# Second layer's output product as Strassen's seven products over 256-token blocks, its weights staged as float32 in DRAM

## The chip, the cores and the metric

One core of a Trainium2 chip runs the kernel. The metric is the device time of one execution in microseconds; the time before is 1062.11 us, the median of three runs. TensorE (PE) multiplies matrices and writes to PSUM; VectorE (DVE), ScalarE (ACT) and GpSimd (POOL) work on elements; SyncE (SP) issues the transfers.

## The reference

Three stages follow each other: a delta-rule attention over 768 steps, and two dense layers over its 3072 tokens.

```python
for t in range(S):                       # S = 768, 4 batches, 8 heads, 48 wide
    y[:, :, t] = einsum('bhd,bhde->bhe', q[:, :, t], state)
    v_old = einsum('bhde,bhd->bhe', state, kt)
    state = state + bt * einsum('bhd,bhe->bhde', kt, vt - v_old)
x = y as [3072, 384]
h = x @ w1_in;  x = (max(h, 0) + log1p(exp(-|h|))) @ w1_out   # 384 -> 2048 -> 384
h = x @ w2_in;  out = (h * cos(h)) @ w2_out                   # 384 -> 2048 -> 384
```

## The kernel before

**Numbers.** Each float32 operand of a product is split into two float16 parts, hi and lo (lo is what hi leaves), and a product is the sum of three matmuls, hi by hi, hi by lo and lo by hi (PAIRS). The weights arrive as 64-bit words; `conv` (L437) loads a 768 KB piece (128 hidden features of both weight matrices), turns it to float32 with three integer operations on DVE and a scaling on ACT or DVE, and makes hi and lo. `weights(0)` and `weights(1)` (L421) do that for the 16 pieces of each layer; `weights(1)` can begin only once the tiles of the attention's preparation are given up (`open_wp2`, L954, key `wp2`).

**Stages.** The attention works in 24 chunks of 32 steps (`step`, L696), prepared four at a time (`norms`, `prep`, `solve`). After two chunks, 256 tokens are ready for the first layer: `moe_block(0, j)`, 12 blocks of 8 units, a unit being two hidden pieces of 128 features. The second layer, `moe_block(1, j)`, runs 6 blocks of 512 tokens by 16 units of one hidden piece. A unit is an input product (`moe_in`, L784), the elementwise work that makes g and its hi and lo, and an output product (`moe_out`, L845) that accumulates in PSUM over the block's units. `moe_end` (L868) empties the accumulators: for the first layer into DRAM (`x2d`), for the second to the output.

**The second layer's unit.** The input product is 9 matmuls (3 pieces of 384 features by 3 pairs) of 128 by 512 into one of five PSUM banks (`hring`). DVE adds and subtracts a magic number (L835, L401), ACT takes the absolute value and the sine (L406, L408), DVE multiplies (L401), ACT or DVE copies hi (`copy`, L385), POOL or DVE subtracts for lo (`tt`, L397). The output product is 9 matmuls of 512 columns (3 pieces of 128 output features by 3 pairs) into three banks (`acc2`).

**Order.** Every operation is handed to `put` with the engines that may run it and an estimated cost, and with the keys that it writes and reads. `Plan` puts all of them into one fixed order per engine before the run, by a list scheduling forwards and backwards over those costs; in its model DVE operations marked `port` and POOL operations exclude each other. At run time each engine follows its order and waits by semaphores. All transfers are issued by SP, in order. The attention has a small priority boost, and the layers fill TensorE between its steps.

## Time and profile before

| | us |
|---|---|
| median of three runs | 1062.11 (1055.21 to 1067.48) |
| the profiled execution, device time | 1063.94 |
| its span in the trace | 1062.1 |
| TensorE busy in the span | 946.3 |
| DVE, ACT, POOL busy | 656.2, 681.4, 404.0 |

The profile shows one execution. Busy times of TensorE's matmuls include the length of its pipeline, so the pace is read from the starts of following instructions, not from their durations. Times in a timeline count from the start of the span. An instruction's line can be that of a helper (L397 is every tensor-tensor operation, L401 every scalar-tensor-tensor, L385 every copy).

### The profile page before, as it was taken

The page shows a single profiled execution, that of the slowest core. Times are in us where ns is not written, and L with a number is a line of the kernel's source. Part 1 is how long each engine was busy: PE and PEld are TensorE (multiplying, and loading weights), DVE is VectorE, ACT ScalarE, POOL GpSimd, SP SyncE. Part 2 cuts the span into 40 slices and gives each one's busy share as a digit, 9 for nine tenths or more (in the row PEclk, how much of TensorE's full clock was granted, in tenths as well). Part 3 has the DMA queues.
Part 4 walks back from the last instruction along what each step waited for, and adds up shares of the span by engine and source line. Part 5 has one row for each costly group of instructions (what it writes and reads, how often), then busy time and mean ns, then how long its engine had stood idle before and what let it go on. Part 6 is the DMA issues. An engine that isn't in the chain of part 4 may idle for free.

```text
span 1062.1 us, 27812 instructions
## 1 busy us (share of the span) xinstructions
PE 946.3 (89%) x11552; PEld 687.3 (65%) x11552; DVE 656.2 (62%) x1146; ACT 681.4 (64%) x1281; POOL 404.0 (38%) x365
## 2 busy tenths in 40 slices
PE   1246769898889899999999999999999999999998
PEld 1146648797778789889988998844444444444443
DVE  7876877566836683674485675497555555555554
ACT  5455748686757676777666877976555545555554
POOL 7363526433423352252223433555223323223332
PEclk9556978999989999999999999999999999999999
DMA  8888794758754876567477972111101000010000
GB/s 246 217 219 173 162 246 113 178 129 181 174 127 69 178 170 121 84 156 168 68 148 178 215 169 83 60 45 60 60 1 60 1 30 30 1 60 1 30 1 31
DMA packets 307742, 117.94 MB, mean 111 GB/s; under 512 B 272160, under 2 KB 287648, under 8 KB 307616
## 3 DMA queue, kind: packets, MB, share of 16 engines
q1 hardware_dynamic: 307616, 116.17, 46.2%
q8 instruction: 91, 1.49, 0.6%
q14 instruction: 35, 0.29, 0.1%
HBM read 71.03 MB, written 35.65 MB: 100 GB/s over the span
## 4 chain that ended last, share of the span: by engine, by line
PE 63%; DVE 9%; DMA 8%; SPq 7%; ACT 6%; issue 4%; POOL 2%; DVEq 0%; POOLq 0%; ACTq 0%
PE psH L798 18%; PE accA L860 12%; PE accB L860 9%; PE psC L798 7%; SPq L376 7%; PE psA L860 6%; PE psC L679 5%; PE psY L798 3%; PE psY L679 2%; DMA kt<-k_dram 2%; DMA bdA<-kq 1%; DMA kpd<-kp 1%; PE psA L589 1%; DVE tmpd L397 1%; DVE tlan L397 1%
## 5 line engine op out<-in xcount | busy, mean ns | idle before, releaser
L397 POOL TENSOR_TENSOR g<-g,g 128x512 f16<-128x512 f32 x192 | 227.4, 1185 | 499.1 <-ACT g L385 489.1
L798 PE MATMUL psH<-xt,w 128*128 128x256 f16 x1728 | 238.2, 278 | 7.6 <-DVE g L397 5.9
L385 ACT ACTIVATE g<-g 128x512 f16<-128x512 f32 x192 | 120.5, 629 | 104.4 <-DVE g L401 65.4
L798 PEld LDWEIGHTS <-w 128*128 128x128 f16 x1728 | 159.5, 99 | 28.3 <-issue 8.1
L860 PEld LDWEIGHTS <-w 128*128 128x128 f16 x1728 | 162.8, 98 | 21.2 <-issue 1.6
L860 PE MATMUL accA<-g,w 128*128 128x256 f16 x1152 | 159.0, 275 | 1.1 <-POOL g L397 1.0
L860 PEld LDWEIGHTS <-v 128*128 128x128 f16 x864 | 84.5, 98 | 102.1 <-issue 0.3
L798 PEld LDWEIGHTS <-v 128*128 128x128 f16 x864 | 84.5, 98 | 101.4 <-issue 0.8
L406 ACT ACTIVATE e<-e 128x512 f32<-128x512 f32 x96 | 60.3, 629 | 84.0 <-DVE e L401 84.0
L397 DVE TENSOR_TENSOR g<-psH,e 128x512 f32<-128x512 f32 x96 | 66.1, 688 | 67.1 <-ACT e L408 59.6
L860 PE MATMUL accB<-g,w 128*128 128x256 f16 x576 | 95.0, 275 | 0.0
L798 PE MATMUL psH<-xu,v 128*128 128x512 f16 x351 | 83.3, 379 | 0.6 <-DVE g L401 0.6
L798 PE MATMUL psC<-xu,v 128*128 128x512 f16 x342 | 81.5, 379 | 0.0
L679 PE MATMUL psC<-b,bdT 128*128 128x48 f16 x1152 | 44.1, 186 | 38.3 <-ACT bdT L385 18.9
L860 PE MATMUL accA<-g,v 128*128 128x512 f16 x288 | 78.0, 379 | 0.0
L860 PE MATMUL accB<-g,v 128*128 128x512 f16 x288 | 77.8, 379 | 0.0
L860 PE MATMUL psA<-g,v 128*128 128x512 f16 x288 | 77.6, 379 | 0.0
L679 PEld LDWEIGHTS <-bdKQ 128*128 128x128 f16 x1840 | 64.9, 99 | 15.1 <-issue 12.8
L815 ACT ACTIVATE e<-psH 128x512 f32<-128x512 f32 x96 | 56.8, 591 | 24.5 <-PE psH L798 23.6
L408 ACT ACTIVATE e<-e,hpi 128x512 f32<-128x512 f32 x96 | 69.1, 721 | 2.9
L679 PEld LDWEIGHTS <-bdT 128*128 128x128 f16 x1152 | 41.6, 99 | 42.2 <-issue 38.0
L679 PEld LDWEIGHTS <-bdA 128*128 128x128 f16 x1680 | 55.1, 99 | 9.1 <-issue 7.2
(128 smaller groups left out, 1550.0 us busy)
## 6 DMA issues: line engine op xcount, KB each, us to landing
bdKQ<-kqd SPq DMA_DIRECT2D x184, 64.0 KB, 2.9
kpd<-kp SPq DMA_DIRECT2D x24, 448.0 KB, 3.9
kqd<-kq SPq DMA_DIRECT2D x20, 512.0 KB, 4.5
raw<-w_dram SPq DMA_DIRECT2D x12, 768.0 KB, 6.0
bdA<-kpd SPq DMA_DIRECT2D x96, 96.0 KB, 3.7
w<-w_dram SPq DMA_DIRECT2D x10, 768.0 KB, 6.3
v<-w_dram SPq DMA_DIRECT2D x10, 768.0 KB, 4.8
qt<-q_dram SPq DMA_DIRECT2D x24, 256.0 KB, 3.7
```

The source lines that it names most:

```text
L376: put([("SP", issue)], w, r, lambda e: nc.sync.dma_start(out=dst, in_=src), dma=eng_us, **kw)
L385: nc.scalar.activation(out=out, in_=in_, func=AF.Copy, scale=scale)
L397: put(var, w, r, lambda e: eng[e].tensor_tensor(out=out, in0=a, in1=b, op=op), port=True, **kw)
L406: nc.scalar.activation(out=out, in_=in_, func=func, scale=scale)
L408: nc.scalar.activation(out=out, in_=in_, func=func, scale=scale, bias=bias)
L589: nc.tensor.matmul(ps[:, h], lhsT=w, rhs=x, start=(i == 0), stop=(i == len(ops) - 1))
L679: nc.tensor.matmul(ps[:, h, 0:D], lhsT=lhs(h), rhs=mov[:, h], start=(first and i == 0 and h == 0), stop=(last and i == len(passes) - 1 and ...
L798: nc.tensor.matmul(hp[:, i] if ph == 0 else hp, lhsT=w[:, l, kc * P:(kc + 1) * P], rhs=xv[:, m * KC + kc], start=(kc == 0 and idx == 0), s ...
L815: nc.scalar.activation(out=ev, in_=hv, func=AF.Abs, scale=sc)
L860: nc.tensor.matmul(acc[c], lhsT=w[:, l, c * P:(c + 1) * P], rhs=rhs, start=(f == 0 and idx == 0 and (ph == 1 or c != 1)), stop=(f == NF - ...
```

## The change

The second layer now works in 12 blocks of 256 tokens by 8 units of two hidden pieces, like the first. Its input product takes 18 matmuls of 256 columns. Its output product is Strassen's scheme over halves of the tokens, of the two hidden pieces, and of the 384 outputs: seven products of 128 tokens by 128 features by 192 outputs instead of eight. Here the combinations of g (`z`, 128 by 128) are the stationary operand and the combinations of the weights (192 columns) the moving one; each product is three matmuls, 21 a unit. They accumulate in seven halves of four banks (`acc2`); four banks are left for the input products. `moe_in` makes five sums or differences of quarters of g (`gx`) and hi and lo of all seven operands; `moe_end` combines the seven accumulators with copies and six multiply-adds into one tile and one 384 KB transfer.

The weights of the second layer: `early2`, put behind `weights` in the first layer, runs the 64-bit to float32 conversion and stores the result in DRAM (`w2d`). `weights2`, put in front of the last block of the first layer, loads it back in pairs of pieces and makes hi and lo of the input weights, the combinations of the output weights and their hi and lo. Several new tiles lie where earlier stages have theirs: the key `late` stands for the end of the attention's use, `late2` for the end of the first layer's use of its g tiles. The output's layout in DRAM becomes token by feature.

```diff
-NB2 = NS // 4
-NT = 2 * P, 4 * P
+NB = NS // 2
+NT = 2 * P
+DH = DM // 2
...
     hring = ([(ps_h[i], [("psH", i)]) for i in range(2)],
-             [(flat[i][0], [flat[i][1]]) for i in (1, 2, 4, 5, 6)])
-    acc2 = [flat[3], flat[7], flat[0]]
+             [(x.rearrange("p (a t) -> p a t", a=2), [k]) for x, k in (flat[i] for i in (1, 2, 4, 5))])
+    acc2 = [flat[i] for i in (0, 6, 3, 7)]
+    spare = bdA2.rearrange("p n b t -> p (n b t)")
+    raw2 = [spare[:, 4 * DM * 2 * i:4 * DM * 2 * (i + 1)].bitcast(I64).rearrange("p (o n) -> p o n", o=2) for i in range(2)]
+    gx = [spare[:, 6144 + 1280 * i:6144 + 1280 * (i + 1)].bitcast(F32).rearrange("p (k t) -> p k t", k=5) for i in range(2)]
+    gx16 = [x[:, 0:14 * P].rearrange("p (m k t) -> p m k t", m=2, k=7) for x in (
+        g16t.rearrange("p n a i t -> p (n a i t)"), bdT.rearrange("p h b t -> p (h b t)"),
+        bdG.rearrange("p h b t -> p (h b t)"))]
...
+    w2d = dr.tile([NFP, P, 2, 2, DM], I32, name="w2d")
...
+    def early2():
+        for f in range(NF):
+            cv, ck = cvb[f % NCV], [("cv", f % NCV)]
+            conv(w2, f, lambda: raws[0], [("raw", 0)], [], lambda cv=cv: cv, ck)
+            dma(w2d[f // 2, :, f % 2], cv, [("w2d", f // 2, f % 2)], ck, 1.09)
...
+    def weights2():
+        WP = [("wp2",)]
+        for p in range(NFP):
+            late = [("late",)] if p > 4 else []
+            at = PLACE[p]
...
+            put([("SP", 0.475)], ck, [("w2d", p, 0), ("w2d", p, 1)] + (WP if at == "x" else [("late",)] if at in "st" else []),
+                lambda e, p=p, pair=pair: nc.sync.dma_start(out=pair(), in_=w2d[p]), dma=2.18)
+            split(lambda p=p: win[0][:, 2 * p:2 * p + 2, 0], lambda p=p: win[0][:, 2 * p:2 * p + 2, 1],
+                  lambda pair=pair: pair().bitcast(F32)[:, :, 0], [("wi", 2 * p), ("wi", 2 * p + 1)], ck + WP + late, 2 * DM)
+            CV = ck + WP + late
...
+            for k, k2, a, b, op in ((0, 2, (A_, A_, 0), (A_, A_, 1), ALU.add), (2, 3, (A_, 0, 0), (A_, 1, 1), ALU.add),
+                                    (3, 4, (A_, 0, 1), (A_, 1, 1), ALU.subtract),
+                                    (4, 5, (A_, 0, 0), (A_, 1, 0), ALU.subtract)):
+                n = (k2 - k) * DH
...
+            for j, (k, n, x, r) in enumerate((
+                    (0, 3, lambda: wtmp[0][:, 0:3], [("wt", 0), ("wt", 2)]), (3, 1, lambda y=y: y((A_, 1, 1)), CV),
+                    (4, 1, lambda y=y: y((A_, 0, 0)), CV), (5, 2, lambda: wtmp[0][:, 3:5], [("wt", 3), ("wt", 4)]))):
...
+                put([("ACT", act(m)), ("DVE", dve(m, True))], key if j == 0 else key[1:], r + WP + late + ([] if j == 0 else key[:1]),
+                    lambda e, hl=hl: hl(e, 0), port=True)
+                put([("POOL", pool(m)), ("DVE", dve(m))], key[1:], r + WP + key[:1], lambda e, hl=hl: hl(e, 1), port=True)
...
+    PROD = ((0, 1), (2, 3), (4, 5), (6,))
...
+            q = gv.rearrange("p f (t n) -> p f t n", t=2)
+            x_, z = gx[s], gx16[s3]
+            L = [("late",), ("late2",)]
+            tt(x_[:, 0:2], q[:, :, 0], q[:, :, 1], ALU.subtract, [("gx", s, 0)], gk + L, 2 * P)
+            tt(x_[:, 3:5], q[:, 0], q[:, 1], ALU.add, [("gx", s, 3)], gk + L, 2 * P)
+            tt(x_[:, 2], q[:, 0, 0], q[:, 1, 1], ALU.add, [("gx", s, 2)], gk + L, P, only=("DVE",))
+            a = gv[:, 0, 0:P]
+            own = AP(a.tensor, a.offset, [a.ap[0], [3 * P, 2], a.ap[1]])
+            XK = [("gx", s, i) for i in (0, 2, 3)]
+            ZK = [("z", s3, i) for i in range(4)]
+            copy(z[:, 0, 5:7], own, 1.0, ZK[:1], gk + L, 2 * P)
+            tt(z[:, 1, 5:7], own, z[:, 0, 5:7], ALU.subtract, ZK[1:2], gk + ZK[:1], 2 * P)
+            copy(z[:, 0, 0:5], x_, 1.0, ZK[2:3], XK + L, 5 * P)
+            tt(z[:, 1, 0:5], x_, z[:, 0, 0:5], ALU.subtract, ZK[3:4], XK + ZK[2:3], 5 * P)
...
+            z = gx16[s3]
+            for (bank, key), ks in reversed(list(zip(acc2, PROD))):
+                def fn(e, bank=bank, ks=ks):
+                    for k in ks:
                         for idx, (l, m) in enumerate(PAIRS):
-                            rhs = g16[:, m, i] if ph == 0 else g16[:, m].rearrange("p a t -> p (a t)")
                             nc.tensor.matmul(
-                                acc[c], lhsT=w[:, l, c * P:(c + 1) * P], rhs=rhs,
-                                start=(f == 0 and idx == 0 and (ph == 1 or c != 1)),
-                                stop=(f == NF - 1 and idx == 2 and (ph == 1 or c != 0)))
-                us = 3 * len(cs) * mm(NT[ph])
+                                bank[:, DH * (k % 2):DH * (k % 2 + 1)], lhsT=z[:, m, k], rhs=wo(u)[:, l, k],
+                                start=(u == 0 and idx == 0 and k == ks[0]),
+                                stop=(u == NFP - 1 and idx == 2 and k == ks[-1]))
+                us = 3 * len(ks) * mm(DH)
                 moe_left[0] -= us
-                put([("PE", us)], [key], [("g16", s3, 0), ("g16", s3, 1), ("w", ph, f, 1)], fn, base=moe_left[0])
+                put([("PE", us)], [key], [("z", s3, i) for i in range(4)] + [("wx", u, i) for i in range(4)], fn,
+                    base=moe_left[0])
...
+            sc = 2.0 * math.pi / (G2_SC * W_SC)
+            o = wbuf[j % 2].bitcast(F32).rearrange("p o n -> p (o n)")[:, 0:2 * DM].rearrange("p (t c) -> p t c", t=2)
+            M = [acc2[k // 2][0][:, DH * (k % 2):DH * (k % 2 + 1)] for k in range(7)]
+            mk = [[acc2[k // 2][1]] for k in range(7)]
+            ok = [[("o", j % 2, i)] for i in range(4)]
+            old = [("w", 2 * (j % 2) + i, a) for i in range(2) for a in range(2)] if j < 2 else []
+            diag = AP(o.tensor, o.offset, [o.ap[0], [DM + DH, 2], [1, DH]])
+            def both(x):
+                return x.unsqueeze(1).to_broadcast([P, 2, DH])
+            copy(diag, both(M[2]), sc, ok[0] + ok[3] + old, mk[2], DM, ps=True)
+            copy(o[:, 0, DH:], M[3], sc, ok[1], mk[3] + ok[0], DH, ps=True)
+            copy(o[:, 1, 0:DH], M[4], sc, ok[2], mk[4] + ok[0], DH, ps=True)
+            for k, sg, dst, qs in ((3, -1, o[:, 0, 0:DH], (0,)), (1, 1, o[:, 0, 0:DH], (0,)), (4, -1, o[:, 1, DH:], (3,)),
+                                   (0, -1, o[:, 1, DH:], (3,)), (5, 1, o[:, :, DH:], (1, 3)), (6, -1, o[:, :, 0:DH], (0, 2))):
+                m = M[k] if len(qs) == 1 else both(M[k])
+                stt(dst, m, sg * sc, dst, ALU.mult, ALU.add, [x for i in qs for x in ok[i]], mk[k], DH * len(qs))
+            dma(out[j], o, [("out", j)], [x for i in ok for x in i], 1.09, issue=0.65)
...
+    weights()
+    early2()
...
+            if n == NS - 1:
+                put([("-", 0.0)], [("late",)] + [x for k in ("bdK", "bdQ", "bdA", "bd2", "bdT", "bdG") for x in bk(k)], (),
+                    lambda e: None)
+                weights2()
...
+    put([("-", 0.0)], [("late2",)] + [("g16", i, k) for i in range(NG16) for k in range(2)], (), lambda e: None)
```

## Rows read from the trace of the kernel before

The groups stand in the order in which the prediction comes to them. Times are microseconds from the span's start; L is a line of the kernel.

**Rows 1.** Busy times on the page: engine, us (share of the span), instructions

```profile
PE 946.3 (89%) x11552; PEld 687.3 (65%) x11552; DVE 656.2 (62%) x1146; ACT 681.4 (64%) x1281; POOL 404.0 (38%) x365
```

**Rows 2.** Windows of 50 us: busy us (instructions) by engine, PEclk, DMA share, GB/s

```profile
350.00:400.00 50.00, 46.01 (x785) 41.24 (x783) 37.16 (x84) 37.35 (x84) 23.42 (x26) 0.97 0.76 177
750.00:800.00 50.00, 50.00 (x233) 22.65 (x232) 26.60 (x40) 26.36 (x41) 13.90 (x12) 1.00 0.04 16
```

**Rows 3.** Timeline of TensorE, 640 to 700 us: start, length, engine, line, operation, count

```profile
641.67 0.57 PE L679 MATMUL psY<-u,bdA 128*128 128x48 f16 x16
642.08 0.49 PE L798 MATMUL psH<-xt,w 128*128 128x256 f16 x3
...
662.84 2.13 PE L798 MATMUL psH<-xt,w 128*128 128x256 f16 x18
664.80 0.82 PE L860 MATMUL accA<-g,w 128*128 128x256 f16 x6
...
697.54 0.81 PE L860 MATMUL accA<-g,v 128*128 128x512 f16 x3
```

**Rows 4.** Timeline of all engines, 1035 us to the end

```profile
1057.08 1.46 PE L860 MATMUL psA<-g,v 128*128 128x512 f16 x6
...
1058.57 0.60 ACT L385 ACTIVATE w<-psA 128x512 f32<-128x512 f32 x1 [0.70 <-PE psA L860]
```

**Rows 5.** Timeline of all engines, 753 to 775 us

```profile
759.23 2.11 PE L798 MATMUL psH<-xu,v 128*128 128x512 f16 x9
...
761.21 0.63 ACT L385 ACTIVATE g<-g 128x512 f16<-128x512 f32 x1 [0.89 <-DVE g L401]
...
761.91 1.16 POOL L397 TENSOR_TENSOR g<-g,g 128x512 f16<-128x512 f32 x1 [2.80 <-ACT g L385]
762.10 0.69 DVE L401 SCALAR_TENSOR_TENSOR e<-e,psH 128x512 f32<-128x512 f32 x1
...
763.11 2.11 PE L798 MATMUL psC<-xu,v 128*128 128x512 f16 x9
763.48 0.72 ACT L408 ACTIVATE e<-e,hpi 128x512 f32<-128x512 f32 x1
```

**Rows 6.** Groups by form, whole span: busy us, mean ns | idle before, releaser

```profile
L860 PEld LDWEIGHTS <-v 128*128 128x128 f16 x864 | 84.5, 98 | 102.1 <-issue 0.3
...
L467 POOL TENSOR_TENSOR v<-cv,v 128x768 f16<-128x768 f32 x16 | 28.3, 1768 | 9.2 <-ACT v L462 9.2
...
L401 DVE SCALAR_TENSOR_TENSOR u<-psC,u 128x384 f16<-128x384 f32 x48 | 26.5, 553 | 38.1 <-ACT u L385 38.0
...
L397 POOL TENSOR_TENSOR kp<-pm,kp 128x256 f16<-128x256 f32 x24 | 18.9, 789 | 29.2 <-ACT kp L385 27.0 <-PE psC L679 2.2
```

**Rows 7.** Timeline of DVE, then POOL, 700 to 740 us

```profile
705.58 1.53 DVE L454 SCALAR_TENSOR_TENSOR cv<-v,cv 128x768 int32<-128x768 int32 x1
...
715.25 0.67 DVE L835 TENSOR_SCALAR e<-psY 128x512 f32<-128x512 f32 x1
715.85 0.94 DVE L454 SCALAR_TENSOR_TENSOR cv<-raw,cv 128x768 int32<-128x768 int32 x1
...
705.14 1.16 POOL L397 TENSOR_TENSOR g<-g,g 128x512 f16<-128x512 f32 x1 [2.26 <-ACT g L385]
```

**Rows 8.** Window of 20 us: busy us (instructions) by engine, PEclk, DMA

```profile
700.00:720.00 20.00, 19.98 (x94) 8.97 (x93) 17.68 (x26) 14.78 (x22) 11.79 (x9) 1.00 0.11 38
```

**Rows 9.** DMA issues on the page: count, KB each, median us to landing

```profile
raw<-w_dram SPq DMA_DIRECT2D x12, 768.0 KB, 6.0
...
out_dram<-w SPq DMA_DIRECT2D x18, 256.0 KB, 2.0
```

**Rows 10.** Instructions on the second layer's weights: ns min/median/max, first and last start

```profile
L439 SPq DMA_DIRECT2D v<-w_dram x10: 328/388/524, 571.4 to 681.2; - x10
```

**Rows 11.** Chain of work that ended last, 300 to 400 us, by line

```profile
by line: SPq L376 21.0%; PE psH L798 15.5%; PE accA L860 9.8%; PE psC L679 8.5%; DMA kpd<-kp 5.3%; PE accB L860 4.9%; DMA kt<-k_dram 3.7%; PE psY L679 3.4%; DMA bdA<-kq 3.3%; issue 3.3%; DMA bdT<-tgd 2.6%; PE psA L589 2.6%; DVE g L397 2.0%;
```

More of the change, by code (lines that the diff above doesn't have):

```diff
@@ L311, in delta_moe_moe_kernel @@
     NG16 = 3
-    g16b = [moe.tile([P, 2, 2, 2 * P], F16, name=f"g16{i}") for i in range(NG16)]
+    g16t = moe.tile([P, NG16, 2, 2, 2 * P], F16, name="g16")
+    g16b = [g16t[:, i] for i in range(NG16)]
     xsb = moe.tile([P, KC, 2 * P], F32, name="xs")
@@ L464, in hi, with flo @@
                 nc.vector.tensor_copy(out=o_, in_=cf)
-        def lo(e):
-            eng[e].tensor_tensor(out=wview(ph, f)[:, :, 1], in0=cf, in1=wview(ph, f)[:, :, 0], op=ALU.subtract)
-        put([("ACT", act(n)), ("DVE", dve(n, True))], wk, ck, hi, port=True)
-        put([("POOL", pool(n)), ("DVE", dve(n))], wk, ck, lo, port=True)
+        def flo(e):
+            (h_, l_), cf = (x() if callable(x) else x for x in (hi, lo)), src()
+            eng[e].tensor_tensor(out=l_, in0=cf, in1=h_, op=ALU.subtract)
@@ new lines, in split, with conv, half, scale @@
+        put([("ACT", act(n)), ("DVE", dve(n, True))], wk, ck, fhi, port=True)
+        put([("POOL", pool(n)), ("DVE", dve(n))], wk, ck, flo, port=True)
+    def conv(w, f, t, key, r, cv, ck):
+        put([("SP", 0.475)], key, r, lambda e: nc.sync.dma_start(out=t(), in_=w[f]), dma=2.18)
+        n = 2 * DM
+        def half(b):
+            return t().bitcast(I32).rearrange("p o (n two) -> p o n two", two=2)[:, :, :, b]
+        put([("DVE", dve(n, True))], ck, key, lambda e: nc.vector.tensor_scalar(
+            cv(), half(1), 0x07FFFFFF, 3, op0=ALU.bitwise_and, op1=ALU.logical_shift_left), port=True)
+        put([("DVE", dve(n))], ck, key, lambda e: nc.vector.scalar_tensor_tensor(
+            cv(), in0=half(1), scalar=-0x40000000, in1=cv(), op0=ALU.bitwise_and, op1=ALU.bitwise_or), port=True)
+        put([("DVE", dve(n))], ck, key, lambda e: nc.vector.scalar_tensor_tensor(
+            cv(), in0=half(0), scalar=29, in1=cv(), op0=ALU.logical_shift_right, op1=ALU.bitwise_or), port=True)
+        def scale(e):
+            x = cv().bitcast(F32)
+            if e == "ACT":
+                nc.scalar.activation(out=x, in_=x, func=AF.Copy, scale=W_SC)
+            else:
+                nc.vector.tensor_scalar_mul(x, x, W_SC)
+        put([("ACT", act(n)), ("DVE", dve(n, True))], ck, [], scale, port=True)
@@ L832, in moe_in @@
             tt(gv, hv, ev, ALU.add, gk, hk + ek, n, only=("DVE",))
+            copy(g16[:, 0], gv, 1.0, [("g16", s3, 0)], gk, n)
+            tt(g16[:, 1], gv, g16[:, 0], ALU.subtract, [("g16", s3, 1)], gk + [("g16", s3, 0)], n)
         else:
@@ L895, in moe_block @@
             x, xk = (lambda: xt2[j % 2]), [("xt2", j % 2)]
-            put([("SP", 0.475)], xk, [("x2d", 2 * j), ("x2d", 2 * j + 1), ("wp2",)],
-                lambda e: nc.sync.dma_start(out=xt2[j % 2], in_=x2d[j]), dma=2.18)
-        NU = (NFP, NF)[ph]
-        for u in range(NU):
+            put([("SP", 0.475)], xk, [("x2d", j), ("wp2",)],
+                lambda e: nc.sync.dma_start(out=xt2[j % 2], in_=x2d[j]), dma=1.09)
+        for u in range(NFP):
             moe_in(ph, j, u, xk, x)
@@ L902, in moe_block @@
                 moe_out(ph, j, u - 2)
-        for u in range(NU - 2, NU):
+        for u in range(NFP - 2, NFP):
             moe_out(ph, j, u)
```

160 lines of the change are left out of this document (87 added, 73 removed).

## The prediction

> **What bounds the kernel now.** I read the page's busy times first, then the windows, then the timeline of one stretch. On the page TensorE is busy 946 of 1062 us and no other engine over 64% [rows 1]. The windows say where that is a limit. At 350 to 400 us TensorE is idle 4 us of 50, because the attention steps wait for each other; at 750 to 800 us it is not idle at all, at granted clock 1.00, the 2.4 GHz level [rows 2]. The second layer is of that second kind: its first output product starts at 697.54 [rows 3], its last six matmuls at 1057.08 [rows 4]. In the timeline the reader should see a strict rhythm: 18 matmuls of 512 columns (9 of the input product and 9 of the output product, between them) from 759.23 to 763.11, one unit of 512 tokens and 128 hidden features in 3.88 us, with ACT, POOL and DVE following inside it [rows 5]. What is taken from TensorE in this stage comes off the end of the kernel, if the others keep up.
>
> **TensorE.** A new unit is 256 tokens by 256 hidden features, the same work, so 96 units stay 96. Its input product is 18 matmuls of 256 columns, a form that the first layer has: 18 from 662.84 to 664.80, 108.9 ns each [rows 3], 1.96 us. Its output product is 7 products by 3 hi/lo pairs, 21 matmuls of 192 columns with a new 128-column weight load each; the trace has no such form. From above it is bounded by the 108.9 ns of 256 columns, from below by the 48-column form, 16 in 0.41 us, 25.6 ns each, each with its own weight load too [rows 3]. 512 columns take 3.88/18 = 215.6 ns, so a column costs (215.6 - 108.9)/256 = 0.417 ns and 192 columns 82.2 ns. That value I take, since the 48-column row shows that loads of this size don't set the pace down to 26 ns. The unit: 1.96 + 21 x 0.0822 = 3.69 us, less than 3.88 by 0.19, and 96 x 0.194 = **18.6 us saved**. At 108.9 ns the unit would be 4.25 us.
>
> A weight load lasts 98 ns in the trace [rows 6], longer than 82. The Trainium skill ("TensorE: Matmul & The Clock Gate", section "LDWEIGHTS (loading the stationary operand)") makes a load columns/1.2 ns, 107 ns for 128. An estimate from that page, with loads one after another: 21 matmuls take 2.25 us, the unit 4.21, and the kernel loses 32 us on TensorE where the rows give 18.6 less. The 48-column row, 25.6 ns with a load each, does not agree with loads in series.
>
> **The other engines in a unit.** DVE keeps its three PSUM operations of 0.69 us [rows 5]. Removed are one 512-element hi copy and one 512-element subtraction. Added are two sums or differences of 256 and one of 128, hi copies of 256 and 640 and subtractions of 256 and 640. On DVE 384 elements take 0.55 us [rows 6] and 512 take 0.69, so 128 are 0.28 (DVE only), 256 are 0.41, 640 are 0.83. On POOL 256 take 0.79, 512 take 1.16 and 768 take 1.77 on average [rows 5, 6], so 640 are some 1.46. ACT: 0.72 for the sine, 0.63 for a 512-element operation [rows 5], hi copies about 0.4 + 0.76 by that: 2.5 us of 3.69, no bound. DVE and POOL hinder each other when DVE reads from SBUF alone: a subtraction on POOL began at 705.14, a weight operation on DVE at 705.58 took 1.53 us, where the same operation took 0.94 at 715.85 [rows 7]. Operations reading PSUM show no such stretch (0.69 beside POOL's 1.16 [rows 5]). So the SBUF operations of both add up. With the 640 subtraction on DVE and the three of 256 on POOL they make 0.28 + 0.83 + 3 x 0.79 = 3.48 us; DVE in all 2.07 + 1.11 + 0.32 (block end, below) = 3.50. Both lie under 3.69, at 95%; counted by starts (0.60 apart behind an operation of 0.67 at 715.25 [rows 7]) DVE is nearer 85%. With all four on POOL they make 0.28 + 3 x 0.79 + 1.46 = 4.11, over it. I take the first: before, at 700 to 720, DVE was busy 17.7 of 20 us and POOL 11.8, and TensorE lost 0.02 [rows 8]. Cost 0; at the other end 96 x (4.11 - 3.69) = 40 us.
>
> **Block ends.** They go from 6 to 12; each now has six multiply-adds from PSUM on DVE (four of 192 elements, by the slope 0.35, two of 384 at 0.55: 2.5 us, 0.32 a unit) and three copies. The next block's outputs begin with the bank of product 6, which is read last, so TensorE's outputs wait 0.35 + 0.55 and two handovers of about 0.25 behind the last product: 1.4 us. Cover: one input product, 1.96 us, ready in one of four banks. I take 0; without cover 11 x 1.4 = 15 us.
>
> **Passage between the layers.** The new tiles lie where the first layer's hi/lo of g and the attention's blocks lay, so all Strassen sums wait (key late2) for the first layer's last output product. Then follow a POOL sum, an ACT copy, a subtraction: 0.79 + 0.76 + 0.83 with handovers of 0.1 [rows 5], about 2.7 us. Cover: two input products with free banks, 3.9 us. I take 1 (the cover may have been used earlier), from 0 to 3.
>
> **The end.** Before, one copy on ACT at 1058.57 and 2.9 us to the end [rows 4]. Now two multiply-adds of 192 and two of 384 on DVE, 1.8 us against 0.6, and one transfer of 384 KB for one of 256, which took 2.0 us [rows 9]; by size 1 more. +2.2, from 1.2 to 3.2.
>
> **Weights, moved.** The second layer's 16 loads and conversions ran from 571 us on [rows 10]; now load, integer work and scaling run under the first layer's matmuls, at most 16 x 3 x 0.94 = 45 us of DVE [rows 7], which is idle 13 us of 50 there [rows 2]. Added are 16 stores of 384 KB and 8 reloads. In place of the late conversions stand 8 pairs of splits and sums, 3072 elements with two inputs each, at 0.69 per 512 some 4 us of DVE, 33 us in all, which POOL can share. The old conversions ran beside the second layer too, and TensorE lost 0.02 of 20 us [rows 8], so nothing is taken for it; without that cover it is 33 us. The price falls before 570: 16 loads and 16 stores stand on SP's queue between the attention's loads of blocks, and that queue is 21% of the chain at 300 to 400 [rows 11]. At 0.39 us an issue [rows 10] 32 issues are 12.5 us of SP; at that share 2.6 lie on the chain; a 768 KB load occupies the transfer engines in front of block loads too (6.0 us to landing [rows 9]). A store waits for ACT's scaling, and behind it, in SP's order, wait block loads, for which TensorE's next attention group waits. I take **4 us**, from -3 (the shorter queue after 570) to 14 (all issues and a little more).
>
> **Sum.** 1063.9 (the profiled execution) - 18.6 + 1 + 2.2 + 4 = 1052.5; the median lies 1.8 below the profiled execution, so **1050.7 us, about 1051** at the median.
>
> **Rivals.**
> - Hidden anyway (chance 0.2): the early conversions cost nothing or the lighter queue helps, 1051 - 4 - 2 = 1045. For it: DVE's idle 13 us.
> - First layer slowed (0.19): the upper end, 14 for 4, and 3 at the passage: 1063, no change. For it: SP's share of the chain.
> - DVE and POOL become the bound (0.17), the other side: midway between 3.69 and 4.11, a unit of 3.90, gives 1051 + 96 x 0.21 = 1071, and at 4.11 it is 1091. From 3.69 + 11.4/96 = 3.81 us a unit on, nothing is left of the gain. For it: 95% by durations; against it: 700 to 720 us. The Trainium skill ("SBUF — State Buffer", section "SBUF: two separate sides") calls the shared port an exclusive lock, held for a whole instruction; the stretched operation at 705.58 agrees.
> - Weight loads set the pace (0.04): at 98 ns the 21 matmuls take 2.06 us, the unit 4.02, and the time is 1051 + 96 x 0.33 = 1083.
> - The forecast: 0.40, with its own range of 1047 to 1057.
>
> **How the numbers follow.** About 1% is what a measurement of this kernel tells from no change: 1051.5 and 1072.7 are the bounds. Faster by more: the 0.2 of hidden anyway, and 0.25 of the forecast's 0.40, whose centre lies just inside: 0.45. Within 1%: the other 0.15, 0.17 of the first layer slowed, 0.05 of the engine bound: 0.37. Slower: 0.12 of the engine bound, 0.04 weight loads, 0.02 of the first layer slowed: 0.18. The range from 1041 to 1074 leaves out the worse part of the engine bound (0.10), weight loads (0.04) and a very good first layer (0.04).
>
> **What would show it.** Right: 192-column matmuls start 82 ns apart and a steady unit takes 3.69 us; TensorE idle under 3 us between 720 us and the end; layer two's first output product at most 5 us later than 697; DVE some 3.3 us a unit. Wrong: idle TensorE in the second layer ended by DVE or POOL (engine bound); starts of 98 ns and more (weight loads); idle TensorE before 600 us well over 4 us in 50, ended by DMA or steps behind SP (first layer).

## The result and the profile after

The changed kernel takes 1071.52 us (median of 11 runs, 1067.42 to 1075.33), the kernel before beside it 1060.97 us: a ratio of 1.0100 with a 95% interval of 1.0075 to 1.0126. It is slower by 1%, where the prediction said 1051 us and faster. The profiled execution took 1074.66 us with a span of 1072.0.

The busy times of the page after, to be held against [rows 1]:

```profile
PE 932.7 (87%) x13568; PEld 854.7 (80%) x13568; DVE 731.8 (68%) x1314; ACT 721.9 (67%) x1419; POOL 653.8 (61%) x709
```

TensorE is busy 13.6 us less (the pace, below, is the better measure of the saving, since a busy time holds the pipeline's length of each group), and yet the span is 9.9 us longer, so its idle time grew by 23.5 us, from 115.8 to 139.3. The windows (length, then busy us and count by engine, PEclk, DMA share, GB/s) say where. First the kernel before, then after:

```profile
0.00:300.00 300.00, 203.15 (x3723) 182.45 (x3724) 216.09 (x416) 194.72 (x409) 143.12 (x137) 0.85 0.76 185
300.00:650.00 350.00, 335.20 (x5789) 304.62 (x5786) 212.19 (x402) 248.42 (x501) 118.81 (x112) 0.99 0.66 142
```

```profile
0.00:300.00 300.00, 202.30 (x3713) 181.33 (x3714) 225.18 (x424) 195.31 (x410) 142.48 (x138) 0.94 0.75 186
300.00:650.00 350.00, 318.62 (x5504) 288.16 (x5502) 221.78 (x412) 240.53 (x485) 116.08 (x113) 0.98 0.74 171
650.00:750.00 100.00, 97.33 (x1032) 88.25 (x1031) 45.24 (x74) 79.73 (x154) 98.33 (x116) 1.00 0.19 63
720.00:1060.00 340.00, 340.00 (x3596) 321.49 (x3594) 262.19 (x439) 225.16 (x406) 321.37 (x375) 1.00 0.08 26
```

Up to 300 us nothing is lost (3723 matmuls before, 3713 after, busy 203.15 and 202.30 us). From 300 to 650 us TensorE does 16.6 us less in the same 350, at nearly the same granted clock. From 720 to 1060 us it is never idle, at granted clock 1.00, the 2.4 GHz level. So 16.6 of the 23.5 us of idle time lie in the attention and the first layer; some 2 follow between 650 and 750 us and some 4 at the end (below), and in between the second layer is as fast as it was meant to be.

**The second layer.** The timeline of TensorE after (start, length, engine, line, operation, count):

```profile
859.80 0.66 PE L970 MATMUL accA<-bdKQ,bdG 128*128 128x192 f16 x6
860.30 0.66 PE L970 MATMUL psY<-bdKQ,bdG 128*128 128x192 f16 x6
860.79 0.66 PE L970 MATMUL psA<-bdKQ,bdG 128*128 128x192 f16 x6
861.29 1.80 PE L885 MATMUL psC<-xu,vi 128*128 128x256 f16 x15
```

Eighteen matmuls of 192 columns start within 1.49 us, 83 ns each. The groups by form, 720 to 1060 us (busy us, mean ns of one, then idle before):

```profile
L419 ACT ACTIVATE e<-e,hpi 128x512 f32<-128x512 f32 x93 | 66.6, 717 | 1.7
L970 PEld LDWEIGHTS <-bdT 128*128 128x128 f16 x651 | 54.9, 98 | 0.9
L408 POOL TENSOR_TENSOR bdA<-g 128x256 f32<-128x256 f32 x187 | 135.8, 741 | 1.5 <-DVE g L412 1.4
L408 POOL TENSOR_TENSOR bdG<-bdA,bdG 128x640 f16<-128x640 f32 x31 | 43.7, 1410 | 6.9 <-ACT bdG L396 6.9
L408 DVE TENSOR_TENSOR bdA<-g 128x128 f32<-128x128 f32 x94 | 65.1, 693 | 9.7 <-POOL bdT L408 3.2 <-POOL g L408 1.7 <-POOL bdG L408 1.4
```

A unit is 39 matmuls, so the 3596 of the window are 92.2 units in 340 us: 3.69 us a unit, as predicted, and 3.88 before [rows 5]. (The window cuts units at both edges, so that it counts 93 sines, one a unit.) The sums of 256 and the subtractions of 256 and 640 elements, however, all run on POOL, which is busy 321.37 of 340 us.

**The first layer.** What DVE waits for, 300 to 660 us after (total us, times, longest; the row heads the list), and TensorE's longest wait there:

```profile
DVE cv L472 <- DMA raw<-w_dram: 30.4, 12, 6.7
...
PE psC L766 <- ACT st L396: 8.0, 4, 4.7
```

Before, DVE's waits for loads of weights in that stretch came to 2.0 us:

```profile
DVE cv L450 <- DMA raw<-w_dram: 2.0, 1, 2.0
```

One of the twelve, in the timeline of all engines after:

```profile
517.77 0.69 DVE L408 TENSOR_TENSOR g<-psH,e 128x512 f32<-128x512 f32 x1 [2.56 <-ACT e L419]
518.14 0.38 SPq L466 DMA_DIRECT2D raw<-w_dram  x1
...
519.81 0.36 PE L766 MATMUL psC<-u,bdA 128*128 128x48 f16 x8
...
521.32 0.82 PE L957 MATMUL accA<-g,w 128*128 128x256 f16 x6
...
525.20 0.56 DVE L472 TENSOR_SCALAR cv<-raw 128x768 int32<-128x768 int32 x1 [6.74 <-DMA raw<-w_dram]
525.68 1.01 DVE L412 SCALAR_TENSOR_TENSOR st<-psC,st 128x384 f32<-128x384 f32 x2
526.26 0.52 ACT L396 ACTIVATE st<-st 128x384 f16<-128x384 f32 x1 [7.14 <-DVE st L412]
...
526.84 0.80 PE L766 MATMUL psC<-st,bdKQ 128*128 128x48 f16 x16 [4.70 <-ACT st L396]
```

DVE finishes at 518.46, and the next instruction in its fixed order is the integer work on a weight piece whose load was issued only at 518.14. It stands there 6.74 us. Behind it in the order is the update of the attention's state (525.68), whose matmuls had ended at 520.17; for that update waits ACT (526.26), and for that TensorE (526.84), idle 4.70 us. Over the whole stretch, 10.0 of TensorE's 31.4 us of idle time from 300 to 650 us lie within DVE's waits for these loads or the 2 us behind them (added up from the trace); the kernel before is idle for 14.8 us of that stretch, none of it at such a wait. Nobody needs that piece soon: the first reload of a stored pair is issued at 583.8 us.

The page's transfers after (KB each, median us to landing) and the chain of waits from 400 to 560 us, by line:

```profile
raw<-w_dram SPq DMA_DIRECT2D x22, 768.0 KB, 6.6
...
w2d<-cv SPq DMA_DIRECT2D x16, 384.0 KB, 5.3
```

```profile
by line: PE psH L885 16.4%; DMA raw<-w_dram 15.7%; SPq L387 10.5%; PE accA L957 10.3%; PE psC L766 6.3%; PE accB L957 5.7%; PE psA L676 3.9%; DMA bdA<-kq 3.7%; PE psY L766 3.1%; issue 2.8%; DMA kpd<-kp 2.0%; DVE u L412 1.8%; DVE g L408 1.7%
```

The plan counts 0.475 + 0.65 + 2.18 + 0.9 = 4.2 us from the issue of such a load to its landing on a free queue; the trace has 6.6, so DVE's turn is planned 2.4 us too early by the transfer alone. In the example the issue was late as well: it came 0.32 us before DVE was free. All 16 early loads share one landing buffer (`raws[0]` in `early2`), so a load can't be issued before the piece ahead of it has been converted.

### The profile page after: what moved, and what is told of

It reads as the page before. It is cut to its first block, busy times and chain, and to the rows that moved or that the text cites. A ratio compares the mean times of both kernels' runs of the same rounds, so it can differ in the third digit from the quotient of the medians.

```text
span 1072.0 us, 32783 instructions
## 1 busy us (share of the span) xinstructions
PE 932.7 (87%) x13568; PEld 854.7 (80%) x13568; DVE 731.8 (68%) x1314; ACT 721.9 (67%) x1419; POOL 653.8 (61%) x709
## 4 chain that ended last, share of the span: by engine, by line
PE 40%; DMA 16%; DVE 12%; POOL 10%; ACT 9%; SPq 7%; issue 5%; DVEq 0%; POOLq 0%; ACTq 0%
PE psH L885 12%; PE psC L885 7%; SPq L387 7%; DMA raw<-w_dram 5%; PE psY L970 4%; PE psA L970 4%; PE accA L970 4%; PE accA L957 3%; POOL g L408 3%; DMA kt<-k_dram 2%; PE psC L766 2%; DMA kpd<-kp 2%; PE accB L970 2%; DMA cv<-w2d 2%; DMA qt<-q_dram 1%
## 5 line engine op out<-in xcount | busy, mean ns | idle before, releaser
L408 POOL TENSOR_TENSOR g<-g,g 128x512 f16<-128x512 f32 (+1 forms) x128 | 137.1, 1071 | 218.7 <-ACT g L396 212.1
L885 PE MATMUL psH<-xt,w 128*128 128x256 f16 x1728 | 232.2, 277 | 8.9 <-DVE g L408 4.1
L885 PEld LDWEIGHTS <-vi 128*128 128x128 f16 x1728 | 167.5, 98 | 19.5 <-issue 2.3
L408 POOL TENSOR_TENSOR bdA<-g 128x256 f32<-128x256 f32 x192 | 139.5, 742 | 1.5 <-DVE g L412 1.4
L885 PE MATMUL psH<-xu,vi 128*128 128x256 f16 x864 | 106.7, 273 | 2.1 <-DVE g L412 2.1
L885 PE MATMUL psC<-xu,vi 128*128 128x256 f16 x864 | 105.9, 273 | 0.0
L396 ACT ACTIVATE g<-g 128x512 f16<-128x512 f32 (+1 forms) x128 | 72.9, 570 | 39.0 <-DVE g L408 32.0
L417 ACT ACTIVATE e<-e 128x512 f32<-128x512 f32 x96 | 60.1, 626 | 40.6 <-DVE e L412 39.8
L766 PEld LDWEIGHTS <-bdT 128*128 128x128 f16 x1152 | 41.4, 98 | 49.1 <-issue 42.6
L408 DVE TENSOR_TENSOR bdA<-g 128x128 f32<-128x128 f32 x96 | 66.2, 690 | 9.8 <-POOL bdT L408 3.2
L419 ACT ACTIVATE e<-e 128x512 f32<-128x512 f32 x96 | 59.8, 623 | 1.0
L970 PEld LDWEIGHTS <-bdT 128*128 128x128 f16 x672 | 56.6, 98 | 3.5 <-POOL bdT L408 2.5
```

Source lines behind the costliest of these rows:

```text
L396: nc.scalar.activation(out=out, in_=in_, func=AF.Copy, scale=scale)
L408: put(var, w, r, lambda e: eng[e].tensor_tensor(out=out, in0=a, in1=b, op=op), port=True, **kw)
L417: nc.scalar.activation(out=out, in_=in_, func=func, scale=scale)
L419: nc.scalar.activation(out=out, in_=in_, func=func, scale=scale, bias=bias)
L766: nc.tensor.matmul(ps[:, h, 0:D], lhsT=lhs(h), rhs=mov[:, h], start=(first and i == 0 and h == 0), stop=(last and i == len(passes) - 1 and ...
L885: nc.tensor.matmul(hp[:, i], lhsT=w[:, l, kc * P:(kc + 1) * P], rhs=xv[:, m * KC + kc], start=(kc == 0 and idx == 0), stop=(kc == KC - 1 a ...
```

## The experiments

Three causes were set against each other: **A**, DVE standing in its order before loads that land later than planned; **B**, the transfers themselves (16 loads of 768 KB and 16 stores of 384 KB, by their issues on SP or by their bytes); **C**, the integer work on DVE. The table gathers all runs: the median, the ratio to the kernel before measured beside it, TensorE's busy us in two windows, and DVE's idle us ended by a load into `raw`, 300 to 660 us, as in the views above.

| kernel | us | ratio [95%] | 300–650 | 650–750 | DVE waits |
|---|---|---|---|---|---|
| before | 1061–1062 | | 335.2 | 99.4 | 2.0 |
| after | 1071.5 | 1.0100 [1.0075, 1.0126] | 318.6 | 97.3 | 30.4 |
| e1_slack | 1067.5 | 1.0049 [1.0026, 1.0073] | 331.7 | 89.0 | 5.4 |
| e2_transfers | 1063.0 | 1.0014 [0.9990, 1.0037] | 325.9 | 99.3 | 0 |
| t1_e2_slack4 | 1062.8 | 1.0014 [0.9990, 1.0038] | 326.3 | 99.7 | 0 |
| e3_no_early | 1047.2 | 0.9864 [0.9822, 0.9906] | 333.6 | 99.2 | 0 |
| t2_e3_order | 1046.8 | 0.9863 [0.9823, 0.9902] | 333.9 | 99.2 | 0 |
| e4_late | 1072.8 | 1.0112 [1.0063, 1.0161] | 341.1 | 83.8 | 6.5 |
| e5_dve_prep | 1062.3 | 1.0007 [0.9988, 1.0026] | 329.8 | 95.3 | 8.1 |
| e6_dve_lo | 1056.5 | 0.9948 [0.9927, 0.9970] | 332.9 | 95.3 | 9.4 |
| s1_e6_slack6 | 1069.2 | 1.0077 [1.0049, 1.0105] | 334.2 | 86.8 | 4.5 |
| e10_no_slack | 1068.1 | 1.0042 [1.0015, 1.0068] | 321.9 | 98.2 | 27.1 |
| e11_mixed | 1055.4 | 0.9934 [0.9910, 0.9958] | 332.3 | 98.1 | 11.2 |
| e7_small | 1052.3 | 0.9920 [0.9891, 0.9949] | 334.6 | 99.2 | 0 |
| e8_work | 1044.4 | 0.9852 [0.9807, 0.9897] | 335.8 | 99.2 | 0 |
| t3_after_slack05 | 1063.2 | 1.0025 [1.0002, 1.0049] | 327.3 | 97.2 | 18.4 |
| h4_half | 1046.8 | 0.9853 [0.9823, 0.9883] | 336.4 | 98.5 | 3.5 |
| s3_h4_slack6 | 1050.9 | 0.9892 [0.9849, 0.9936] | 335.1 | 97.3 | 1.8 |
| h6_quarter | 1062.7 | 1.0010 [0.9986, 1.0033] | 330.8 | 93.6 | 1.0 |
| s2_h6_slack6 | 1051.6 | 0.9895 [0.9838, 0.9953] | 338.8 | 91.2 | 1.0 |

### Undoing parts of the weights' move

**No early work at all** (e3_no_early): the early loop is gone, and the late reloads read other data of the same size.

```diff
-    early2()
...
-                lambda e, p=p, pair=pair: nc.sync.dma_start(out=pair(), in_=w2d[p]), dma=2.18)
+                lambda e, p=p, pair=pair: nc.sync.dma_start(out=pair().rearrange("p f o n -> p (f o n)").rearrange("p (a x) -> p a x", a=3), in_=q[3 * p:3 * p + 3].rearrange("a p x -> p a x").bitcast(I32)), dma=2.18)
```

> The early loads, conversions and stores are all left out; the 8 later reloads take the same number of bytes from the q input instead (the second layer computes with other weights). This is the floor of the first layer beside Strassen: all theories 1046-1054, by the 18 us saved on TensorE. A and C: within 4 us of the run with transfers alone. B: 13 us or more below that run.

1047.2 us. Strassen's products, their sums and the reloads together bring 14.8 us (1061.98 to 1047.19); the prediction's terms without the weights were -18.6 + 1 + 2.2 = -15.4. The run also leaves out the conversions, which the kernel before has, but e8_work below has them again and is no slower. So the early part costs 1071.5 - 1047.2 = 24.3 us in the order of the kernel after.

**Transfers without the integer work** (e2_transfers): each early piece is loaded, and the store writes what lies in the other tile; it waits for the load, so that the buffers are used in the same order.

```diff
-            conv(w2, f, lambda: raws[0], [("raw", 0)], [], lambda cv=cv: cv, ck)
-            dma(w2d[f // 2, :, f % 2], cv, [("w2d", f // 2, f % 2)], ck, 1.09)
+            put([("SP", 0.475)], [("raw", 0)], [], lambda e, f=f: nc.sync.dma_start(out=raws[0], in_=w2[f]), dma=2.18)
+            dma(w2d[f // 2, :, f % 2], cv, [("w2d", f // 2, f % 2)], ck + [("raw", 0)], 1.09)
```

> All 16 early loads and 16 early stores stay, with the same sizes, but the integer operations and the scaling between them are left out (the stores write the first layer's last converted weights, so the second layer computes with other weights). A: DVE has nothing to wait for, 1050-1057. B: still slow, 1066-1073. C: 1050-1057, like A.

**The same issues with 24 KB each** (e7_small), on top of e3_no_early:

```diff
+            put([("SP", 0.475)], [("raw", 0)], [], lambda e, f=f: nc.sync.dma_start(out=raws[0][:, 0, 0:48], in_=w2[f][:, 0, 0:48]), dma=0.14)
+            dma(w2d[f], cv[:, 0, 0:48], [("w2d", f)], ck + [("raw", 0)], 0.07)
...
```

> No conversions, reloads from q as in the run without early work; the 16 early loads and 16 stores are issued on SP, but with 24 KB each in place of 768 and 384 (the second layer computes with other weights). Theory F (the transfers' cost, 16 us between the runs with transfers alone and without, is their bytes in front of the attention's block loads): 1047-1051. Theory G (it is the 32 issues on SP's queue, with the waits of a store for its load): 1058-1064.

**The integer work without the transfers** (e8_work), on top of e3_no_early: the conversion runs on what lies in the tile.

```diff
-        put([("SP", 0.475)], key, r, lambda e: nc.sync.dma_start(out=t(), in_=w[f]), dma=2.18)
+        if w is not w2:
+            put([("SP", 0.475)], key, r, lambda e: nc.sync.dma_start(out=t(), in_=w[f]), dma=2.18)
...
-            dma(w2d[f // 2, :, f % 2], cv, [("w2d", f // 2, f % 2)], ck, 1.09)
...
```

> The 16 early conversions' operations on DVE and ACT run, on what lies in the landing buffer, but nothing is loaded or stored early; reloads from q as in the run without early work. Theory C (the work itself slows the attention): 1054-1060. If the work is hidden in DVE's idle time: 1046-1050.

C falls: with all integer work and no transfer the kernel takes 1044.4 us (below the 1046 to 1050 expected), no more than without it, though DVE is busy 35 us more (230.06 us from 300 to 650 against 195.43). The transfers alone cost 15.8 us (1062.96 - 1047.19), the 32 issues with few bytes only 5.1, in the one order that was run. By these runs two thirds of B are bytes: from 300 to 650 us the DMA engines are busy 0.60 of the time without the transfers and 0.75 with them. The time of e2_transfers lies between what A and C expected and what B expected, and e7_small between its two theories, nearer to the bytes. TensorE's waits there, 300 to 650 us, first without and then with the transfers:

```profile
PE psA L675 <- DMA bdA<-kq: 4.1, 3, 1.7
```

```profile
PE psA L676 <- DMA bdA<-kq: 8.9, 3, 5.3
PE psC L766 <- ACT u L396: 5.6, 2, 3.2
PE psY L766 <- ACT u L396: 5.5, 1, 5.5
```

The attention's small loads come later, and the steps after them. What B costs in the kernel after is not measured by this: without the integer work the plan puts the transfers earlier (the stores are issued from 157.6 to 526.7 us, in the kernel after from 315.6 to 629.4), and a store waits on SP for its load where in the kernel after it waits for the scaling.

### Planning the loads later

**The early loads planned 4 us later** (e1_slack): no instruction is added, only the order that is worked out from the planned landing changes.

```diff
-            conv(w2, f, lambda: raws[0], [("raw", 0)], [], lambda cv=cv: cv, ck)
+            conv(w2, f, lambda: raws[0], [("raw", 0)], [], lambda cv=cv: cv, ck, slack=4.0)
```

> Only the planner's idea of the early loads changes: each of the 16 early weight loads is planned to land 4 us later than it was, so the conversions stand later in DVE's fixed order; work, transfers and buffers are the same. Theory A (DVE, in order, stands still for loads that land later than planned, 30 us at 300 to 660 us in the changed kernel, and the attention steps queue behind it): DVE's idle time before the first integer operation falls below 10 us at 300 to 660, and the time falls from 1071 to 1053-1060. Theory B (the extra transfers and issues on SP's queue delay the attention's block loads): 1067-1074. Theory C (the 45 us of integer work on DVE delay the steps, whenever they stand): 1067-1074.

```profile
300.00:650.00 350.00, 331.74 (x5767) 302.79 (x5763) 225.69 (x420) 251.43 (x506) 117.88 (x115) 0.99 0.75 170
650.00:750.00 100.00, 89.03 (x830) 79.55 (x829) 45.54 (x75) 70.32 (x135) 98.60 (x119) 0.97 0.19 64
```

DVE's waits fall from 30.4 to 5.4 us, and TensorE wins 13.1 of its 16.6 us back. Only 4 us of that reach the end, so that the time misses A's range of 1053 to 1060 and lies in that of B and C, though the waits did what A expected: 8.3 are lost again between 650 and 750 us, where POOL is busy 98.6 of 100 us and DVE 45.5. TensorE's waits there:

```profile
PE psH L885 <- DVE g L412: 4.1, 1, 4.1
PE accB L970 <- POOL bdT L408: 3.2, 1, 3.2
PE accB L970 <- POOL bdG L408: 1.5, 1, 1.5
PE accA L970 <- POOL bdT L408: 1.2, 1, 1.2
```

**That stretch relieved**, on top of e1_slack: e5_dve_prep puts the late weights' subtractions and sums on DVE alone, e6_dve_lo also the 640-element subtraction of each unit, and e11_mixed gives the late subtractions free to POOL again.

```diff
-        put([("POOL", pool(n)), ("DVE", dve(n))], wk, ck, flo, port=True)
+        put([x for x in (("POOL", pool(n)), ("DVE", dve(n))) if x[0] in lo_on], wk, ck, flo, port=True)
...
-            tt(z[:, 1, 0:5], x_, z[:, 0, 0:5], ALU.subtract, ZK[3:4], XK + ZK[2:3], 5 * P)
+            tt(z[:, 1, 0:5], x_, z[:, 0, 0:5], ALU.subtract, ZK[3:4], XK + ZK[2:3], 5 * P, only=("DVE",))
```

> The longer planned landing of the early loads, and besides: the second layer's late weight work (sums, hi/lo subtractions in weights2) may run on DVE alone, not on POOL. Theory D (with the landing planned, the 14 us that the attention wins back are lost again in the passage, because POOL does nearly all of the late weight work and the Strassen sums, busy 98.6 of 100 us at 650 to 750, while DVE is busy 45): POOL falls to 70-85 there, TensorE idles under 3 us instead of 11, and the time is 1056-1061. Rival E (the passage waits for the weights' transfers and order, whichever engine works on them): 1064-1069.

> As the run before, and besides the 640-element subtraction of every unit of the second layer on DVE alone, as the prediction had counted it. If POOL, busy 48 of 50 us in the second layer, costs something at the passage and at the end (2.7 us of TensorE idle after 1060 in the changed kernel): 2-5 us below the run before. If it costs nothing: within 1.5 us. If DVE and POOL then block each other at their port: 5-20 us above.

> As e6_dve_lo, but the hi/lo subtractions of the late weight work may run on POOL again; the sums of weights and the 640-element subtractions stay on DVE. In e6_dve_lo DVE is busy 91 of 100 us at 650 to 750 and POOL 46, and TensorE idles 4.7 us. If that is now DVE's doing: 1052-1055. If not: 1055-1059.

From 1067.5 the time goes to 1062.3, then 1056.5 and 1055.4 us (the first 1.3 us above its range of 1056 to 1061, the second 5.8 us faster where 2 to 5 was the most expected). The windows of e6_dve_lo:

```profile
300.00:650.00 350.00, 332.88 (x5776) 303.54 (x5776) 230.74 (x430) 249.29 (x501) 108.87 (x106) 0.98 0.76 171
650.00:750.00 100.00, 95.32 (x926) 86.05 (x924) 90.67 (x154) 76.36 (x147) 45.99 (x50) 1.00 0.20 68
```

Read with e1_slack: POOL's 98.6 us become 46.0, DVE's 45.5 become 90.7, and TensorE has 6.3 us more. e11_mixed has all transfers and all work of the kernel after (with the 640-element subtraction on DVE) and is 8.2 us over e3_no_early: in that order and split the move costs some 8 and not 24. The 8 would be more if the split also helped a kernel without the early part, which no run shows.

**The landing planned early again** (e10_no_slack), on top of e6_dve_lo:

```diff
-            conv(w2, f, lambda: raws[0], [("raw", 0)], [], lambda cv=cv: cv, ck, slack=4.0)
+            conv(w2, f, lambda: raws[0], [("raw", 0)], [], lambda cv=cv: cv, ck)
```

> The run e6_dve_lo without its longer planned landing: late weight work and the 640-element subtractions on DVE alone, the early loads planned as in the changed kernel. Theory A (DVE's waits in order for loads planned too early cost the attention some 14 us, hidden until now by the passage): 1066-1072, with 25 us or more of DVE idle before the first integer operation at 300 to 660. Rival (the two DVE edits brought all of the gain, the planned landing little): 1055-1060.

```profile
DVE cv L472 <- DMA raw<-w_dram: 27.1, 11, 5.5
```

```profile
300.00:650.00 350.00, 321.87 (x5522) 290.68 (x5521) 217.98 (x421) 242.91 (x488) 107.63 (x102) 0.97 0.72 166
```

The waits are back, and with them the loss: 11.0 us of TensorE in that stretch, 11.6 us in the median. TensorE's idle time within the waits or the 2 us behind them is 10.3 us, in e6_dve_lo 0.5. This supports A in the first layer, as far as one order against one other can.

**How far one order may be trusted.** Kernels were run again in another fixed order, by other planned landings alone: e6_dve_lo as s1_e6_slack6 (6 us for 4), e2_transfers as t1_e2_slack4 (4 for 0), e3_no_early as t2_e3_order (2 for 0, on the late reloads). t3_after_slack05 is the kernel after with 0.5 us, so that most of the waits stay. The first and the last as diffs:

```diff
-            conv(w2, f, lambda: raws[0], [("raw", 0)], [], lambda cv=cv: cv, ck, slack=4.0)
+            conv(w2, f, lambda: raws[0], [("raw", 0)], [], lambda cv=cv: cv, ck, slack=6.0)
...
-            conv(w2, f, lambda: raws[0], [("raw", 0)], [], lambda cv=cv: cv, ck)
+            conv(w2, f, lambda: raws[0], [("raw", 0)], [], lambda cv=cv: cv, ck, slack=0.5)
```

> e6_dve_lo with 6 us of planned landing added instead of 4: the same work, only another fixed order. If named causes carry the differences between the runs: 1054-1059, DVE's idle time before the first integer operation not above e6's. If the fall of the order alone moves the time by several us: outside of that, with the loss in a stage where no wait on loads stands.

> The run with early transfers alone, in another order: its loads planned to land 4 us later. If transfers alone have a price of some 10 us or more: 1058-1066. If the 16 us of the first such run were mostly its order: 1048-1055.

> The run without early work, in another order: the 8 reloads planned to land 2 us later. If its 1047.2 is what Strassen gives with nothing else in the first layer: 1043-1051. If it was a lucky order: above 1053.

> The changed kernel in another order that keeps the fault: its early loads planned to land 0.5 us later, still some 3 us too early. Theory A: DVE idles 20 us or more before the first integer operation at 300 to 660, TensorE's busy time there is 12 us or more below that of the kernel before, and the time is 1066-1074. If the changed kernel was one unlucky order: under 1062.

The two kernels without waits hold still: e2_transfers and t1_e2_slack4 differ by 0.1 us, e3_no_early and t2_e3_order by 0.4. That is the firmest number here, the transfers alone at 16 us in both orders. The others move: s1_e6_slack6 is 12.7 us slower than e6_dve_lo, with fewer waits and a good first layer (334.2): its last load is issued at 638.4 us (617.8 in the kernel after), and at the passage TensorE waits 4.9 and 4.4 us for the second layer's weights (86.8 of 100). t3_after_slack05 still has 18.4 us of waits and 6.5 us of idle TensorE at them, and takes 1063.2 us, below its range of 1066 to 1074. That is the time of e2_transfers, which has no such wait, so the end time of this pair shows no price of the waits. Another order changes more than the waits: the first early store is issued at 315.6 us in the kernel after, at 209.2 in e1_slack, 180.2 in t3_after_slack05. Over all kernels with the whole early part the rule in the first layer holds: 18 to 30 us of waits go with 318.6 to 327.3 us of TensorE, 4 to 11 us with 329.8 to 334.2, and the kernel without the early part has 333.6. The end of the kernel doesn't follow as well, since the passage at 650 to 750 us differs by up to 11.

### Less of it early

**Nothing early, all converted late** (e4_late): no copy in DRAM; the pieces are loaded as 64-bit words and converted beside the second layer's begin, as in the kernel before.

```diff
-    PLACE = "crxcrcrc"
+    PLACE = "cccccccc"
...
-    early2()
...
+            for i in range(2):
+                conv(w2, 2 * p + i, lambda: raws[0], [("raw", 0)], [], lambda i=i: cvb[i], [("cv", i)])
```

> Strassen alone: the 64-bit weights are loaded and converted late, in pairs in front of the splits, as before the change (no float32 copy in DRAM). A: the first layer is as fast as before; the conversions, with one landing buffer and about 16 us a pair, crowd the passage between the layers from 575 to 720 us: 1052-1064. B: 1050-1060. C: the same 45 us of DVE fall where TensorE has a backlog: 1050-1060.

```profile
300.00:650.00 350.00, 341.09 (x5887) 312.75 (x5883) 217.83 (x403) 259.01 (x527) 145.54 (x144) 1.00 0.62 133
650.00:750.00 100.00, 83.80 (x717) 71.70 (x716) 70.36 (x91) 64.88 (x118) 82.77 (x89) 0.88 0.20 71
```

The first layer is the fastest of all, 341.1 of 350, and the passage the worst, 83.8 of 100, with the granted clock down to 0.88: 1072.8 us, where all three theories expected 1050 to 1064. Conversion, sums, hi and lo of the weights then all fall into that stretch.

**Half early** (h4_half): e6_dve_lo with 8 pieces early and 8 loaded as 64-bit words and converted late, as in e4_late; three of these land in two buffers beside `raws[0]`.

```diff
-        for f in range(NF):
+        for f in range(8):
-    PLACE = "crxcrcrc"
+    PLACE = "rxrxcccc"
+    LAND = 'rrrr01r0'
...
```

> As e6_dve_lo, but only the first 8 of 16 pieces go the way over DRAM in the first layer; the other 8 are loaded as 64-bit words and converted late, in front of their splits. If the early bytes are what costs (11 of 16 us between transfers alone and none, by the run with small ones), half of them saves 5 to 8 us at 150 to 550; the late conversions add 20 us of DVE to a passage where it is busy 91 of 100: 1050-1060, and where TensorE idles tells which of the two it was.

> h4_half with 6 us instead of 4. If halving the early bytes is what brought h4 to 1046.8: 1045-1051. If it was a lucky order: 1052-1060.

```profile
300.00:650.00 350.00, 336.36 (x5739) 306.29 (x5735) 232.27 (x455) 255.51 (x518) 109.47 (x104) 0.98 0.69 158
650.00:750.00 100.00, 98.47 (x974) 89.66 (x972) 88.40 (x145) 75.98 (x138) 54.75 (x60) 1.00 0.09 30
```

1046.8 us, below its range of 1050 to 1060, and 1050.9 in a second order (s3_h4_slack6), within 1045 to 1051: faster than both kernels, by 1.5% and 1.1% against before. It computes everything and comes out at the time of e3_no_early, which leaves the early part out.

**Three quarters early** (h6_quarter) and its second order (s2_h6_slack6):

```diff
-        for f in range(8):
+        for f in range(12):
-    PLACE = "rxrxcccc"
-    LAND = 'rrrr01r0'
+    PLACE = "crxcrrcc"
+    LAND = 'rr01'
...
```

> As h4_half with 12 pieces early and 4 late: 2.5 to 4 us less in the first layer, 10 us more DVE work in the passage: 1051-1058.

> h6_quarter with 6 us instead of 4. h6 measured 1062.7, where 1051-1058 was expected from fewer early bytes. If its extra loss is an unlucky fixed order: 1050-1058. If 4 late conversions have a price of their own (TensorE idles 6.4 us at 650 to 750): 1060-1065 again.

1062.7 and 1051.6 us: the first is 4.7 us above its range of 1051 to 1058, the second in it, and the two orders lie 11 us apart, so it says nothing on how the cost grows with the bytes.

## Why the prediction was wrong

**The step that failed** is the term "Weights, moved", +4 us with bounds of -3 and 14. It measured 24.3 (after less e3_no_early), and with it the sum would have been 1050.7 + 20.3 = 1071.0; in the order of t3_after_slack05 it is 16.0, above the bound of 14 too. The mechanism that the prediction named, a store or a load in front of block loads, exists: 16 us with the transfers alone. It was priced by SP's share of the chain, 2.6 us of issues; e7_small shows issues at 5.1, and the bytes, 19 MB (16 of 768 KB and 16 of 384 KB) in a stretch whose DMA engines were 0.66 busy already, were given almost nothing. The second half wasn't seen at all: the prediction counted DVE's idle time as cover for the integer work, and it is (e8_work), but it didn't ask whether the data would be there when DVE's turn came, and 10.0 us of TensorE's idle time in the first layer lie at those waits. An engine that follows a fixed order gives its idle time away at the place where the order puts the waiting instruction. The prediction named what is queued behind an added wait on SP, but not on DVE. How the 24.3 us split between transfers and waits in the kernel after stays open: these runs don't change the waits without the order, e2_transfers puts the transfers at 16 us in its own place and order, and e11_mixed the whole move at some 8 once the waits are down to 11 us.

**The rivals.** The time of 1071 us is the one given for "DVE and POOL become the bound", and that is not what happened: TensorE had 340.00 of 340 us. "First layer slowed" has the place, and its price of 14 was too low by 10. "Hidden anyway" gave 1045, about what the kernel takes without the early part (1047.2, and 1044.4 with its integer work).

**What held.** The pace: 83 ns a matmul for 82.2, 3.69 us a unit as predicted. The Trainium skill ("TensorE: Matmul & The Clock Gate", section "LDWEIGHTS (loading the stationary operand)") gives 107 ns for a load of 128 columns; the loads last 98 ns in the trace, and yet the matmuls behind them start every 83, so loads don't come one after another with the matmuls here, and the estimate of 32 us lost, which took them so, is not borne out.

**What came out right by luck.** The 640-element subtraction was taken to be on DVE; the plan put all four on POOL. That was priced at 4.11 us a unit and a loss of 40. On POOL the two sums took 0.74 each and the 640 elements 1.41 (rows above), the subtraction of 256 elements 0.67. The timelines after, first POOL and then DVE:

```profile
849.41 0.67 POOL L408 TENSOR_TENSOR bdT<-g,bdT 128x256 f16<-128x256 f32 x1
...
853.72 1.40 POOL L408 TENSOR_TENSOR bdG<-bdA,bdG 128x640 f16<-128x640 f32 x1 [0.22 <-ACT bdG L396]
```

```profile
849.88 0.35 DVE L408 TENSOR_TENSOR bdA<-g 128x128 f32<-128x128 f32 x1
...
853.83 1.43 DVE L408 TENSOR_TENSOR bdA<-g 128x128 f32<-128x128 f32 x1
```

That is 3.56 us of POOL, or 3.49 by its busy time (321.37/92.2), under the 3.69 of TensorE. DVE's 128-element sum takes 0.35 us at 849.88 and 1.43 at 853.83, beside POOL's 1.40, and 0.69 on average. In both rows it ends 0.14 to 0.15 us behind the POOL operation that was running when it began; of the 94 sums 89 begin beside such an operation, and 82 of these end 0.14 to 0.15 us behind it, while the other five take 0.28 to 0.29. So more than half of a sum's length is waiting, and adding the sum's 0.28 to POOL's time, as the prediction did, gives 3.49 + 0.28 = 3.77, over the 3.69 that a unit took. The Trainium skill ("SBUF — State Buffer", section "SBUF: two separate sides") calls the port between both an exclusive lock, held for a whole instruction, and the rows agree. DVE had room for the stretch, at 262 us of 340. The 0.79 of [rows 6] was a mean over another stage's operations and too high.

**Passage and end.** The passage costs one wait of 2.1 us in front of the first output product (predicted 1, up to 3):

```profile
718.73 0.49 PE L885 MATMUL psH<-xu,vi 128*128 128x256 f16 x3 [2.08 <-DVE g L412]
719.05 0.41 PE L970 MATMUL accB<-vo,g 128*128 128x192 f16 x3
```

That product was to start at most 5 us later than 697; it starts at 719.05, behind the first layer's loss. At the end the rows after are:

```profile
1066.74 0.41 PE L970 MATMUL accB<-bdKQ,bdG 128*128 128x192 f16 x3
...
1067.98 0.55 DVE L412 SCALAR_TENSOR_TENSOR w<-accA,w 128x384 f32<-128x384 f32 x1
1068.59 0.33 SPq L387 DMA_DIRECT2D out_dram<-w  x1
```

From the last matmul's start, 1066.74 + 2 x 0.083 = 1066.91, to the end of the span are 5.1 us; before they were 3.9 (six from 1057.08 at 0.2156 [rows 4], end at 1062.1). That is +1.2, the lower bound of the term of 2.2. Not foreseen were 2.7 us in which TensorE waits for POOL after 1060 us, in the last units, where no later one is left to fill them.
